# Weight maxima ahead of their scale, the second batch beside the conversion, and q by whole rows, in a linear-attention and two-layer feed-forward kernel

## The chip, the cores and the metric

The kernel runs on one core of a Trainium2 chip, as one program. The metric is the device time of that program in microseconds; several runs are taken and their median counts. TensorE (PE in the profile), VectorE (DVE), ScalarE (ACT), GpSimd (POOL) and the DMA queue of SyncE (SP) are programmed side by side. Each works through its own instructions in order and waits for the others by semaphores.

## The reference

```
q, k, v: (8 batches, 8 heads, 576, 64) f32      g_norm: (64)
kv  = einsum('bhsd,bhse->bhde', k, v)
out = einsum('bhsd,bhde->bhse', q, kv)
out = out / sqrt(mean(out * out, axis=-1) + 1e-6) * g_norm
x   = out.transpose(0, 2, 1, 3).reshape(4608, 512)
h = x @ w_in   (512 x 2048);  g = max(0.01 * h, h);   x = g @ w_out   (2048 x 512)
h = x @ w2_in  (512 x 2048);  g = h - tanh(h);        x = g @ w2_out  (2048 x 512)
```

The four weight matrices, w1 to w4 in the kernel, come as 64-bit floats. They are read as pairs of 32-bit words.

## The kernel before

**Products.** Each of the four large products works on 2 x 2 blocks by the seven-product scheme (`NOP = 7`). An operand has seven forms, four sums of blocks and three plain blocks. Each form is split into a high and a low float16 part, and three matmuls, high by high, high by low and low by high, stand for one float32 matmul. In the first product there are 64 steps (8 batches of 576 tokens by 8 pairs of weight blocks), and a step is 7 products of 6 matmuls of 288 columns, all recorded at line 513 as `ps_a` to `ps_d`. The stationary operand is a weight tile `w`. The moving one is `opa`, the three plain forms of x, or `ops`, the four sums of x, each in two halves of the contracted dimension (`kk` 0 and 1). Of the first three products that PE issues in the stream, two read `opa` and the third reads `ops`.

**Attention.** Heads go in pairs, four pairs to a batch. A pair loads k, v and q, and then PE makes kv of two heads (`pk`, 12 matmuls of 64 columns, each head in its own 64 of the 128 output partitions), transposes q in two halves (`pq`, three transposes each, both heads at once), multiplies (`po`, two matmuls of 288 columns in float32), and for every second pair sums the squares (`pm`, four matmuls of 288 columns, each in its own 32 output partitions). ACT and DVE move the results from PSUM. Batch 0 and three pairs of batch 1 run ahead of the first product. The other 25 pairs are cut into six steps that stand between products of the first 64 steps. After a batch's four pairs its root mean squares go through ACT (`iv`, L929), DVE (reciprocal, L937), DRAM and back broadcast over partitions (`bc`), and POOL scales x with them (L952). Then come high and low parts of `opa` (L452, L459), sums on POOL (L491) and the parts of `ops`.

**w1.** Its 16 units of 128 x 512 are loaded as words (L315), ACT takes absolute values of the high words (L329), and DVE takes their maximum (L333) and builds float32 from the words (L340, L346, L352). The maximum over all 16 units gives one power-of-two scale: DVE reduces (L265 to L274), PE transposes `pt` and broadcasts `pb`, DVE ends with `s1g` (L280). Only then are w1's parts made: per unit ACT makes the high and DVE the low part of three plain blocks (128 x 384), POOL makes the four sums in place, ACT and DVE split them (128 x 512; L378, L381). The other weights take the same way during the earlier products, through DRAM.

**Order.** `Plan` is a list of events by planned time with guessed durations. `on_pe` lays PE's work end to end from `plan.pe`, which starts at `START`; `chain` and `do` fit the others into free time of their engine. Instructions are issued in the order of planned times, so the plan decides each engine's order and the hardware the times. `FIRST` and `OFFS` say at which count of products the steps of a pair are put in:

```
    START = last + 45.0
    FIRST = {1: (-18.0, -11.5, -5.0, 5), 2: (18, 29, 39, 50), 3: (64, 75, 86, 97)}
    OFFS = (1, 4, 6, 8, 10, 13)
    order += [("w",) + u for u in UNITS[4:]]
    D_KV, D_Q, D_O, D_M = 0.9, 0.5, 0.6, 0.7
```

## Time and profile before

| | us |
|---|---|
| median of 3 runs | 1518.32 (1515.48 to 1521.1) |
| the profiled execution's own time | 1515.43 |
| its span | 1513.7 |
| PE busy | 1440.1 (95%) |
| DVE busy | 1248.8 (83%) |
| ACT busy | 914.5 (60%) |
| POOL busy | 687.4 (45%) |
| busy share of PE in the first two slices of 37.8 us | 5 and 2 tenths |

Shares are of the span. A matmul's record reaches from its start to its modelled end and overlaps the next one, so a busy PE is not a PE at its peak; the distance of two starts is what one costs in a row. All times in the text are microseconds from the span's start.

### The profile page before, as it was taken

To read this page: it belongs to the slowest core of one execution; us is meant where nothing else is said; L and a number is where in the kernel's file an instruction comes from. 1 tells how busy PE (TensorE), PEld (TensorE's weight loads), DVE (VectorE), ACT (ScalarE), POOL (GpSimd) and SP (SyncE) were. 2 spreads that over 40 slices of the span, in tenths; PEclk is the share of its full clock that TensorE was granted. 3 is DMA by queue.
4 is the path that set the end of the run, shared out by engine and by line. 5 is a ranking of instruction groups with operands and counts; after the bars stand their busy time and mean duration, and the time that the engine had idled before them with its cause. 6 is when DMAs were issued, how large, how long until landed. Compare 5 with 4: busy or idle time off the path is not lost. (4 is left out here: it accounts for less than half of the span.)

```text
span 1513.7 us, 32951 instructions
## 1 busy us (share of the span) xinstructions
PE 1440.1 (95%) x12658; PEld 1192.3 (79%) x12658; DVE 1248.8 (83%) x2019; ACT 914.5 (60%) x1525; POOL 687.4 (45%) x646
## 2 busy tenths in 40 slices
PE   5299999999899999999999999999998999999998
PEld 3167777777677777777777888888887888888887
DVE  4885777787777899999997888978999988888871
ACT  5377777777667645445543677778887554445540
POOL 0474330452542455445442355558885643444430
PEclk8589999999999999999999999999999999999999
DMA  9829998999978845555645866546768644444431
GB/s 265 202 62 249 289 297 247 312 281 328 305 243 283 327 154 186 199 176 176 202 162 189 320 220 211 205 169 223 266 246 300 240 156 144 146 147 141 143 96 36
DMA packets 188926, 323.17 MB, mean 214 GB/s; under 512 B 54112, under 2 KB 130912, under 8 KB 188768
## 3 DMA queue, kind: packets, MB, share of 16 engines
q1 hardware_dynamic: 188768, 321.06, 65.9%
q8 instruction: 99, 1.62, 0.4%
q14 instruction: 59, 0.48, 0.1%
HBM read 190.84 MB, written 130.15 MB: 212 GB/s over the span
## 5 line engine op out<-in xcount | busy, mean ns | idle before, releaser
L513 PEld LDWEIGHTS <-w 128*128 128x128 f16 x8400 | 819.6, 98 | 204.0 <-issue 29.7
L491 POOL TENSOR_TENSOR gl<-gl 128x256 f32<-128x256 f32 (+1 forms) x272 | 297.0, 1094 | 368.9 <-DVE gl L491 142.2
L513 PE MATMUL ps_a<-ops,w 128*128 128x288 f16 (+1 forms) x2400 | 330.9, 282 | 6.7 <-ACT u L564 4.8
L513 PE MATMUL ps_c<-ops,w 128*128 128x288 f16 (+1 forms) x2352 | 315.3, 282 | 12.2 <-DVE g L575 12.2
L513 PE MATMUL ps_a<-opa,w 128*128 128x288 f16 (+1 forms) x2016 | 283.8, 281 | 0.2
L513 PEld LDWEIGHTS <-ops 128*128 128x128 f16 x1728 | 169.1, 98 | 21.6 <-issue 2.0
L513 PE MATMUL ps_b<-opa,w 128*128 128x288 f16 (+1 forms) x1200 | 175.5, 283 | 0.0
L491 DVE TENSOR_TENSOR gl<-gl 128x256 f32<-128x256 f32 (+1 forms) x272 | 151.5, 558 | 4.3
L1249 POOL TENSOR_TENSOR g<-g,th 128x512 f32<-128x512 f32 x72 | 113.3, 1574 | 82.1 <-ACT th L1246 68.8
L513 PEld LDWEIGHTS <-opa 128*128 128x128 f16 x1296 | 126.8, 98 | 14.7
L461 DVE SCALAR_TENSOR_TENSOR ops<-gl,inv,ops 128x1024 f16<-128x1024 f32 x72 | 102.9, 1429 | 29.4 <-ACT ops L454 29.3
L952 POOL TENSOR_TENSOR xg<-xg,bc 128x1152 f32<-128x1152 f32 x16 | 47.4, 2967 | 174.7 <-DMA bc<-iv 125.7
L454 ACT ACTIVATE ops<-gl,inv 128x1024 f16<-128x1024 f32 x72 | 82.4, 1144 | 62.9 <-POOL gl L491 62.9
L452 ACT ACTIVATE ops<-gl 128x1152 f16<-128x1152 f32 x64 | 74.3, 1161 | 74.8 <-POOL gl L491 72.8
L575 DVE SCALAR_TENSOR_TENSOR g<-ps_c,u 128x288 f32<-128x288 f32 x128 | 58.1, 454 | 50.3 <-PE ps_c L513 48.5
L459 DVE TENSOR_TENSOR ops<-gl,ops 128x1152 f16<-128x1152 f32 x64 | 93.5, 1461 | 4.8 <-ACT ops L452 4.7
L513 PE MATMUL ps_c<-w,ops 128*128 128x256 f16 x864 | 97.3, 273 | 0.2 <-DVE osb L575 0.2
L513 PE MATMUL ps_a<-w,ops 128*128 128x256 f16 x864 | 95.8, 273 | 1.4 <-ACT c L566 1.4
L566 ACT ACTIVATE u<-ps_a,up 128x256 f32<-128x256 f32 x144 | 68.1, 473 | 47.1 <-PE ps_a L513 43.4
L378 ACT ACTIVATE wo<-unit,s_w 128x384 f16<-128x384 f32 (+1 forms) x96 | 63.1, 662 | 52.3 <-DVE unit L392 45.5
L491 POOL TENSOR_TENSOR x1g<-x1g 128x256 f32<-128x256 f32 x72 | 65.3, 908 | 49.4 <-DVE opa L461 43.0
L381 DVE SCALAR_TENSOR_TENSOR wo<-unit,s_w,wo 128x384 f16<-128x384 f32 (+1 forms) x96 | 84.8, 891 | 1.6 <-ACT wo L378 1.4
(126 smaller groups left out, 2171.0 us busy)
## 6 DMA issues: line engine op xcount, KB each, us to landing
g<-g SPq DMA_DIRECT2D x64, 576.0 KB, 6.4
gl<-g SPq DMA_DIRECT2D x64, 576.0 KB, 4.7
g<-g SPq DMA_DIRECT2D x72, 512.0 KB, 3.3
gl<-g SPq DMA_DIRECT2D x72, 512.0 KB, 4.4
wd<-wo SPq DMA_DIRECT2D x48, 448.0 KB, 3.3
w<-wd SPq DMA_DIRECT2D x24, 896.0 KB, 7.4
words<-in_moe_w_in_dram SPq DMA_DIRECT2D x64, 256.0 KB, 6.2
words<-in_moe_w_out_dram SPq DMA_DIRECT2D x64, 256.0 KB, 4.8
```

The lines of the kernel that those rows point to most:

```text
L378: nc.scalar.activation(out=dst()[:, 0, a:b], in_=cols(0, n), func=AF.Identity, scale=scale())
L381: nc.vector.scalar_tensor_tensor(out=dst()[:, 1, a:b], in0=cols(0, n), scalar=scale(), in1=dst()[:, 0, a:b], op0=ALU.mult, op1=ALU.subtract,)
L452: nc.scalar.activation(out=o, in_=i_, func=AF.Copy)
L454: nc.scalar.activation(out=o, in_=i_, func=AF.Identity, scale=scale())
L459: nc.vector.tensor_tensor(out=o, in0=i_, in1=h, op=ALU.subtract)
L461: nc.vector.scalar_tensor_tensor(out=o, in0=i_, scalar=scale(), in1=h, op0=ALU.mult, op1=ALU.subtract)
L491: lambda: e.tensor_tensor(out=g()[:, o], in0=g()[:, a], in1=g()[:, b], op=op),
L513: nc.tensor.matmul(out=out_, lhsT=a, rhs=c, start=start and m == 0, stop=stop and m == n - 1, skip_group_check=not fresh,)
L566: nc.scalar.activation(out=t, in_=src, func=AF.Identity, scale=self.scale)
L575: nc.vector.scalar_tensor_tensor(out=o, in0=src, scalar=self.minus if sub else self.scale, in1=t, op0=ALU.mult, op1=ALU.add,)
L952: e.tensor_tensor(out=x, in0=x, in1=held[kk].ap[:, n0:n1], op=ALU.mult)
L1249: e.tensor_tensor(out=g()[:, n], in0=g()[:, n], in1=held["t"].ap[:, n], op=ALU.subtract)
```

## The change

- **q** is loaded like k and v, two heads in one DMA of 1536-byte rows, where two DMAs of 256-byte runs stood. Since the heads are now apart, each half of q is turned by six float32 matmuls with the identity, three for each head, which write the head's own 64 partitions (`tile_position`), where three transposes of both heads stood.
- **w1, scale.** Units of blocks 5, 6 and 7 (`LATE`, 6 of 16) no longer go through the conversion ahead of the scale: DVE takes their maximum from the words (`most`), and the words stay in their buffers; absolute value, clamp, shift and the two joins come after the scale. Units of blocks 0 and 1 (`SOON`) have their sums made by POOL ahead of the scale.
- **All weights, parts.** The seven forms lie side by side in one float32 unit (128 x 896). The sums are made in float32 first, then ACT makes all high parts in one instruction and DVE all low parts in one, where two of each stood (`parts`; the form numbers in `PROD` follow).
- **Batch 0** has its reciprocal in one instruction of 288 columns, and its broadcast by eight float32 matmuls of 288 columns with a 0-1 matrix (`wide`), from which DVE scales x; its sums of x are made by DVE as well. DRAM, POOL and the two broadcasting loads are left out for this batch.
- **Batch 1.** Its first pair is loaded ahead of w1's last two units, the others right behind them. Three pairs still stand ahead of the product stream, the fourth at its head, and later pairs 3 or 4 products earlier. `START` is no longer 45 us behind the last pair of batch 0, but behind the third of batch 1.
- **Plan.** Where a product was planned before what it needs, the kernel stopped; now a trial run of the plan finds out by how much and delays PE's planned time there. No instruction comes of that. The guessed duration of half a q (0.5) is unchanged.

```diff
-PROD = {1: (6, 5), 2: (4, 4), 3: (0, 6), 4: (5, 0), 5: (3, 1), 6: (1, 2), 7: (2, 3)}
+PROD = {1: (6, 4), 2: (4, 3), 3: (0, 5), 4: (5, 0), 5: (3, 1), 6: (1, 2), 7: (2, 6)}
...
+    def count(n):
+        converted[n] += 1
+        if converted[n] == 2 * NP:
+            weight_scale(n, plan.now + 1.0)
+
+    def convert(n, i, kk, t, land, keep=None, later=None, then=()):
...
+        def most():
+            nc.vector.tensor_reduce(
+                out=mw[:, n, 2 * i + kk:2 * i + kk + 1], in_=held["w"].ap[:, 1::2].bitcast(F32), axis=AX.X, op=ALU.max,
+                apply_absolute_value=True,
+            )
+            count(n)
+
+        def clamp():
+            o = held["ap"]
+            nc.vector.tensor_scalar(out=o, in0=o, scalar1=LEAST_HIGH, scalar2=None, op0=ALU.max)
+
+        if later is not None:
+            plan.chain(t, [(None, land, load), ("V", 0.65, most)])
+            later.append([
+                (None, 0.0, room), ("A", 0.7, one), ("V", 0.42, clamp), ("V", 0.42, shift), ("V", 0.69, low), ("V", 0.69, high),
+            ])
+            return
...
+    def sums(w, minus4, merged=False):
...
+    def parts(w, dst, scale):
+
+        def cols():
+            return w().rearrange("p (o c) -> p o c", c=P)
+
+        def hi():
+            nc.scalar.activation(out=dst()[:, 0], in_=cols(), func=AF.Identity, scale=scale())
+
+        def lo():
+            nc.vector.scalar_tensor_tensor(
+                out=dst()[:, 1], in0=cols(), scalar=scale(), in1=dst()[:, 0], op0=ALU.mult, op1=ALU.subtract,
+            )
+
+        return [("A", 1.15, hi), ("V", 1.25, lo)]
...
-            apart = nm != "q"
-            held[nm] = L.take([CP, 2, NC, D] if apart else [CP, NC, 2, D], F32, nm)
-            if apart:
-                nc.sync.dma_start(
-                    out=held[nm].ap.rearrange("p h c d -> p h (c d)"),
-                    in_=src[b, 2 * c:2 * c + 2].rearrange("h (p c) d -> p h (c d)", p=CP),
-                )
-                continue
-            for h in range(2):
-                nc.sync.dma_start(out=held[nm].ap[:, :, h], in_=src[b, 2 * c + h].rearrange("(p c) d -> p c d", p=CP))
+            held[nm] = L.take([CP, 2, NC, D], F32, nm)
+            nc.sync.dma_start(
+                out=held[nm].ap.rearrange("p h c d -> p h (c d)"),
+                in_=src[b, 2 * c:2 * c + 2].rearrange("h (p c) d -> p h (c d)", p=CP),
+            )
...
-                nc.tensor.transpose(
-                    qt[r][0][:, CP * a:CP * a + CP], two_heads(held["q"], r * NC // 2 + a), ident[:CP, :CP]
-                )
+                for h in range(2):
+                    nc.tensor.matmul(
+                        out=qt[r][0][D * h:D * h + D, CP * a:CP * a + CP], lhsT=held["q"].ap[:, h, r * NC // 2 + a],
+                        rhs=ident[:CP, :CP], start=True, stop=True, tile_position=(0, D * h), skip_group_check=True,
+                    )
...
+        def wide(kk, n):
+            k_ = (4 * kk + n) % 4
+            if k_ in used:
+                raise NoRoom("bank")
+            held["b", kk, n] = bank(k_, "pb")
+            nc.tensor.matmul(
+                out=held["b", kk, n][:, :T1], lhsT=hot["t"].ap[:, kk, n], rhs=held["iv"], start=True, stop=True,
+            )
+
+        def scale_wide(kk, n):
+            x = xg[b, kk].ap[:, n]
+            nc.vector.tensor_tensor(out=x, in0=x, in1=held["b", kk, n][:, :T1], op=ALU.mult)
+            free((4 * kk + n) % 4)
...
+            if b == 0:
+                for kk in range(2):
+                    for n in range(4):
+                        plan.chain(
+                            plan.now + 0.2 + 0.7 * (4 * kk + n),
+                            [(None, 0.9, lambda kk=kk, n=n: wide(kk, n)), ("V", 0.46, lambda kk=kk, n=n: scale_wide(kk, n))],
+                        )
+                return
...
+    SOON = (0, 1)
+    LATE, EARLY, GAP = (5, 6, 7), 3, 0.0
...
-        order += [("w",) + u for u in UNITS[hp:hp + 1]]
-    order += [("w",) + u for u in UNITS[4:]]
-    ta = {}
+        order += [("w",) + u for u in UNITS[2 * hp:2 * hp + 2]]
+    order += [("w",) + u for u in UNITS[8:14]] + [("a", 1, PAIRS[0])] + [("w",) + u for u in UNITS[14:]]
+    order += [("a", 1, PAIRS[hp]) for hp in range(1, 4)]
...
+            later = after_scale.setdefault(o[1:], []) if o[1] in LATE else None
+            convert(0, o[1], o[2], t, 5.5, place_w1(o[1], o[2]), later, sums_first(*o[1:]) if o[1] in SOON else [])
...
+                plan.chain(plan.now + 1.3 * kk, ([] if i in SOON or i in LATE else sums_first(i, kk)) + split_first(i, kk))
...
+            if i in LATE:
+                for kk in range(2):
+                    last_ = [(None, 0.0, lambda i=i: pair_(i))] if kk else []
+                    when(
+                        ("w", 0, i - 3, 0), plan.now + 0.3 + STEP * (i - 1) + 2.3 * kk,
+                        lambda i=i, kk=kk, last_=last_: plan.chain(plan.now, after_scale[i, kk][0] + sums_first(i, kk) + last_),
+                    )
+                continue
...
-    START = last + 45.0
+    last = ta[1, PAIRS[0]][0]
+    for hp in range(EARLY):
+        early_pair(1, PAIRS[hp], last + 0.8, ta[1, PAIRS[hp]][1])
+        last += 6.0
+    START = last + GAP
...
-    FIRST = {1: (-18.0, -11.5, -5.0, 5), 2: (18, 29, 39, 50), 3: (64, 75, 86, 97)}
...
+    FIRST = {1: (None,) * EARLY + (0, 8, 16, 24)[:4 - EARLY], 2: (14, 25, 36, 47), 3: (60, 72, 84, 96)}
+    OFFS = {1: (0, 2, 3, 4, 6, 8)}
```

On PE, ahead of the product stream, the rows of before from w1's scale to the third pair of batch 1 (`pt` and the first `pb` are the scale's, `kvd` the two heads' kv):

```order
L234 MATMUL pt<-ident,m_w_690 1x128
L834 MATMUL pk<-v,k 64x64 x12
L244 MATMUL pb<-diag_w_708,ones 128x1
L854 MATMUL pq<-ident,q 128x96 x6
L870 MATMUL po<-qt,kvd_325 128x288 x2
L834 MATMUL pk<-v,k 64x64 x12
L854 MATMUL pq<-ident,q 128x96 x6
L870 MATMUL po<-qt,kvd_326 128x288 x2
L907 MATMUL pm<-sq,sel 32x288 x4
L834 MATMUL pk<-v,k 64x64 x12
L854 MATMUL pq<-ident,q 128x96 x6
L870 MATMUL po<-qt,kvd_325 128x288 x2
```

The same place now (`pb<-iv,hot` is the broadcast of batch 0; four more of these and the first pair's `pk` and `pq` stand ahead of the first row):

```order
L1096 MATMUL pb<-iv,hot 128x288
L992 MATMUL po<-qt,kvd_327 128x288
L1096 MATMUL pb<-iv,hot 128x288
L992 MATMUL po<-qt,kvd_327 128x288
L1096 MATMUL pb<-iv,hot 128x288
L329 MATMUL pt<-ident,m_w_750 1x128
L1096 MATMUL pb<-iv,hot 128x288
L954 MATMUL pk<-v,k 64x64 x12
L339 MATMUL pb<-diag_w_765,ones 128x1
L975 MATMUL pq<-ident,q 64x96 x12
L992 MATMUL po<-qt,kvd_328 128x288 x2
L1029 MATMUL pm<-sq,sel 32x288 x4
```

One pair of batch 1 moved from behind the scale's `pt` to ahead of it, and seven of the eight broadcasts stand ahead of it too.

In the product stream, one half of a q among products on PE, before:

```order
L513 LDWEIGHTS w_0_746
L513 MATMUL ps_c<-ops,w_0_746 128x288
L854 MATMUL pq<-ident,q 128x96 x3
L513 LDWEIGHTS w_2_825
L513 MATMUL ps_a<-opa,w_2_825 128x288
```

And now:

```order
L637 LDWEIGHTS w_0_814
L637 MATMUL ps_a<-ops,w_0_814 128x288
L975 MATMUL pq<-ident,q 64x96 x6
L637 LDWEIGHTS w_1_863
L637 MATMUL ps_a<-opa,w_1_863 128x288
```

Three instructions on all 128 output partitions became six on 64 of them, alone between products. There are 50 such places in the stream before and after.

On DVE, the last 12 rows up to the second half of the low parts of `ops` before:

```order
L459 TENSOR_TENSOR ops<-xg,ops 128x576
L381 SCALAR_TENSOR_TENSOR w_0_746<-w1f_388,s1g,w_0_746 128x384
L459 TENSOR_TENSOR ops<-xg,ops 128x576
L381 SCALAR_TENSOR_TENSOR w_1_780<-w1f_469,s1g,w_1_780 128x384
L381 SCALAR_TENSOR_TENSOR w_0_746<-w1f_388,s1g,w_0_746 128x512
L885 COPY xg<-po 128x288
L381 SCALAR_TENSOR_TENSOR w_1_780<-w1f_469,s1g,w_1_780 128x384
L885 COPY xg<-po 128x288
L381 SCALAR_TENSOR_TENSOR w_2_825<-w1f_527,s1g,w_2_825 128x384
L459 TENSOR_TENSOR ops<-xg,ops 128x576
L381 SCALAR_TENSOR_TENSOR w_0_746<-w1f_388,s1g,w_0_746 128x512
L459 TENSOR_TENSOR ops<-xg,ops 128x576
```

And now (L614 is a sum of x, L519 a low part of w1, L473 the clamp of a late unit, L705 takes a product's result out of PSUM):

```order
L614 TENSOR_TENSOR xg<-xg 128x288 x2
L705 SCALAR_TENSOR_TENSOR g<-ps_b,c_926 128x288
L519 SCALAR_TENSOR_TENSOR w_1_863<-w1f_462,s1g,w_1_863 128x896
L614 TENSOR_TENSOR xg<-xg 128x288
L581 TENSOR_TENSOR ops<-xg,ops 128x576
L519 SCALAR_TENSOR_TENSOR w_2_949<-w1f_541,s1g,w_2_949 128x896
L581 TENSOR_TENSOR ops<-xg,ops 128x576
L519 SCALAR_TENSOR_TENSOR w_2_949<-w1f_541,s1g,w_2_949 128x896
L581 TENSOR_TENSOR ops<-xg,ops 128x576
L473 TENSOR_SCALAR w1f_966<-w1f_966 128x512
L519 SCALAR_TENSOR_TENSOR w_3_971<-w1f_602,s1g,w_3_971 128x896
L581 TENSOR_TENSOR ops<-xg,ops 128x576
```

The low parts of w1 stand among the parts of `ops` as before, now in whole units, and the sums of x have come to DVE; the first result of a product is taken out ahead of the first low part of `ops`. From `s1g` to the last of these rows DVE has 7 low parts of w1 (128 x 896), 8 sums of x, 2 low parts of `opa` of 288 and 2 of 576 columns, 4 of `ops` of 576, 4 copies, 1 scaling of x, 1 result of a product and 1 clamp.

## Rows read from the trace of the kernel before

**Rows 1.** PE, what precedes the products: start, length, instruction, idle before and its releaser
```profile
64.91 0.37 PE L234 MATMUL pt<-ident,m_w 128*1 128x128 f32 x1 [29.18 <-DVE m_w L274]
71.45 1.55 PE L834 MATMUL pk<-v,k 96*64 96x64 f32 x24
...
84.69 1.65 PE L513 MATMUL ps_a<-opa,w 128*128 128x288 f16 x6
86.13 1.59 PE L513 MATMUL ps_b<-opa,w 128*128 128x288 f16 x6
87.61 0.65 PE L513 MATMUL ps_a<-ops,w 128*128 128x288 f16 x4
```
**Rows 2.** ACT and POOL in the same stretch
```profile
45.15 0.66 ACT L329 ACTIVATE w1f<-words 128x512 f32<-128x512 f32 x1 [0.76 <-DMA words<-in_moe_w_in_dram]
55.17 8.71 POOL L952 TENSOR_TENSOR xg<-xg,bc 128x1152 f32<-128x1152 f32 x2 [53.86 <-DMA bc<-iv]
```
**Rows 3.** DVE in the same stretch
```profile
39.52 0.75 DVE L937 RECIPROCAL iv<-iv 128x96 f32<-128x96 f32 x1
...
64.12 0.16 DVE L265 TENSOR_REDUCE m_w<-mw 128x1 f32<-128x16 f32 x1
...
68.44 0.75 DVE L280 TENSOR_TENSOR s1g<-s_w,gcol 128x1 f32<-128x1 f32 x1
...
81.28 0.75 DVE L381 SCALAR_TENSOR_TENSOR w<-w1f,s1g,w 128x512 f16<-128x512 f32 x1 [0.17 <-ACT w L378]
81.95 1.28 DVE L459 TENSOR_TENSOR ops<-xg,ops 128x576 f16<-128x576 f32 x1
...
86.49 0.46 DVE L885 COPY xg<-po 128x288 f32<-128x288 f32 x1 [1.40 <-ACT sq L876]
```
**Rows 4.** Stretches: their ends, length, busy time by engine, granted clock, DMA share, GB/s
```profile
30.00:44.00 14.00, 4.45 (x15) 1.81 (x15) 13.84 (x34) 10.14 (x20) 0.00 (x0) 0.50 1.04 332
64.90:80.60 15.70, 14.51 (x106) 9.26 (x106) 12.56 (x22) 9.13 (x21) 13.37 (x17) 0.50 0.77 157
391.30:398.10 6.80, 5.70 (x26) 3.87 (x26) 6.73 (x12) 5.92 (x14) 5.30 (x6) 0.50 1.15 273
```
**Rows 5.** PE in the product stream, near 97 us
```profile
97.00 0.41 PE L854 MATMUL pq<-ident,q 96*128 96x96 f32 x3
97.25 0.90 PE L513 MATMUL ps_c<-ops,w 128*128 128x288 f16 x6
97.99 0.90 PE L513 MATMUL ps_b<-opa,w 128*128 128x288 f16 x6
98.72 0.65 PE L870 MATMUL po<-qt,kvd 128*128 128x288 f32 x2
99.21 0.90 PE L513 MATMUL ps_a<-ops,w 128*128 128x288 f16 x6
```
**Rows 6.** PE in the product stream, near 150 us
```profile
148.28 0.90 PE L513 MATMUL ps_a<-ops,w 128*128 128x288 f16 x6
149.11 0.69 PE L907 MATMUL pm<-sq,sel 128*32 128x288 f32 x8
149.74 0.91 PE L513 MATMUL ps_a<-opa,w 128*128 128x288 f16 x6
150.48 0.90 PE L513 MATMUL ps_c<-ops,w 128*128 128x288 f16 x6
151.31 0.92 PE L834 MATMUL pk<-v,k 96*64 96x64 f32 x24
152.16 0.91 PE L513 MATMUL ps_a<-opa,w 128*128 128x288 f16 x6
```
**Rows 7.** Group of PE's instructions from 84.6 to 600 us: count, busy, mean ns
```profile
L854 PE MATMUL pq<-ident,q 96*128 96x96 f32 x150 | 21.2, 250 | 0.0
```
**Rows 8.** Later stretches, columns as in rows 4
```profile
168.00:480.00 312.00, 302.28 (x2706) 232.82 (x2704) 238.57 (x446) 223.93 (x442) 117.03 (x116) 0.99 0.92 286
1120.00:1200.00 80.00, 71.89 (x635) 62.64 (x634) 78.29 (x103) 55.98 (x85) 49.82 (x42) 0.98 0.83 295
```
**Rows 9.** PE and ACT around 390 us
```profile
392.24 1.12 PE L513 MATMUL ps_a<-ops,w 128*128 128x288 f16 x4 [4.13 <-ACT u L564]
390.41 0.92 ACT L452 ACTIVATE opa<-xg 128x864 f16<-128x864 f32 x1 [7.56 <-DMA wf<-unit]
```
**Rows 10.** DMA from 5 to 29 us
```profile
DMA packets 9589, 6.48 MB, mean 270 GB/s; under 512 B 5046, under 2 KB 9588, under 8 KB 9588
```

More of the change, by code (lines that the diff above doesn't have):

```diff
@@ L111, in on_pe, with go, miss, met @@
     def on_pe(self, dur, fn):
-        self.at(self.pe, fn)
+        k = self.ops
+        self.ops += 1
+        self.pe += self.delays.get(k, 0.0)
+        def go():
+            self.op = k
+            fn()
+            self.op = None
+        self.at(self.pe, go)
         self.pe += dur
         return self.pe
+    def miss(self, key):
+        if not self.dry or self.op is None and self.first is None:
+            raise AssertionError(("planned too late", self.now, key))
+        if self.first is None:
+            self.first = self.op, key, self.now
+        raise Missed
+    def met(self, key):
+        if self.first and self.first[1] == key:
+            raise Resolved
     def run(self):
@@ L189, in body, with done @@
     done_ = set()
+    def done(*what):
+        for x in what:
+            done_.add(x)
+            plan.met(x)
     def need(what):
-        assert what in done_, ("planned too late", plan.now, what)
+        if what not in done_:
+            plan.miss(what)
     def when(what, t, fn):
@@ L440, in load_weights, with left_stages @@
         )
-    def left_stages(g, dst, scale, T, done=None, first=None, pieces=1, rest=None, gps=None):
+    def left_stages(g, dst, scale, T, over=None, first=None, pieces=1, rest=None, gps=None):
         f = T / 1000.0
@@ L502, in part @@
         kind = "A" if a >= 4 else "S"
-        assert kind in ops.get("ready", ""), ("planned too late", plan.now, kind)
+        if kind not in ops.get("ready", ""):
+            plan.miss(("part", id(ops), kind))
         return ops["A"].ap[:, h, a - 4] if a >= 4 else ops["S"].ap[:, h, a]
@@ L546, in bank @@
             need = {6: "c1", 7: "u2", 3: "22", 4: "u3" if self.one4 else None}.get(p)
-            assert need is None or need in self.done, ("planned too late", plan.now, need)
+            if need is not None and need not in self.done:
+                plan.miss((id(self), need))
             start = p in (1, 2, 5) or p == 4 and not self.one4
@@ L584, in add @@
             if which != "c" or blk == "12":
-                used.discard(self.banks[which])
+                free(self.banks[which])
             if self.ready:
@@ L595, in add_alone @@
             for which in "bc":
-                used.discard(self.banks[which])
+                free(self.banks[which])
             if self.ready:
```

277 lines of the change are left out of this document (161 added, 116 removed).

## The prediction

> **What bounds the kernel now.** I read the stretches first, then PE's timeline, then what PE waits for. From the first product at 84.69 to the end PE hardly rests, so the time is the start of that stream plus what stands in it. In the stream PE is idle in two places worth naming: 312 less 302.28, that is 9.7 us, between 168 and 480 us, and 8.1 us between 1120 and 1200 [rows 8].
>
> Ahead of the stream PE is bound by order and by others. The last words of w1 are there at 45.15 [rows 2], but DVE first finishes all conversions and then stands behind POOL, which scales batch 0's x from 55.17 for 8.71 us [rows 2]; so w1's scale begins at 64.12 [rows 3]. Its transpose starts on PE at 64.91 after 29.18 us of idleness, and three pairs of batch 1 follow at the lower level of the clock (0.50 of 2.4 GHz is 1.2 GHz, [rows 4]), so that the first product comes at 84.69 and the third, the first that needs `ops`, at 87.61 [rows 1]. The two products ahead of it are 86.13 less 84.69 and 87.61 less 86.13, 1.44 and 1.48 us apart, twice the 0.74 us of a product at full clock (149.74 to 150.48, [rows 6]).
>
> **The change, part 1: the head of the stream.** The order of DVE keeps its reciprocal where it was, at 39.52 [rows 3]; three pieces of 0.75 us in one, less what each piece needs to start, are some 2.1 us, so PE can begin the broadcasts at 41.6. A float32 matmul of 288 columns costs 0.49 us at full clock (98.72 to 99.21, [rows 5]), so 0.98 us at half, at which the clock stands after so long a rest [rows 4]. Seven broadcasts (6.9 us) and a pair (at most 71.45 less 64.91, 6.5 us, with two small matmuls of the scale in it, [rows 1]; 6.0 taken) stand ahead of `pt`: 54.5 us. The words are no bound: with one pair of batch 1 (0.885 MB, 2.7 us at 332 GB/s, [rows 4]) ahead of the last two units they land by 48 us. From `pt` to `s1g` it was 64.91 to 68.44 plus 0.75, 4.3 us [rows 1, 3]; a broadcast and a `pk` now stand in between, 1.0 and 1.5 us: `s1g` at 61.3. Two pairs follow on PE, 6.5 us each at half the clock and half of it at full, so the first product starts at 65 to 71, middle 67.5, against 84.69.
>
> That is not yet the gain, for the third product waits for `ops`. From `s1g` to there DVE has 30 instructions in its order: 7 low parts of 896 columns, of which no row exists (0.75 us for 512 [rows 3], in proportion 1.31; 1.15 taken, since part of an instruction is fixed), 8.0 us; 16 of 288 columns at 0.46 [rows 3], 7.4 us; 6 of 576 columns, 1.28 with POOL at work beside DVE [rows 3], twice 0.46 as the low end, 0.8 taken because POOL has no work of batch 0 now, 4.8 us; the clamp 0.45. That is 20.7 us, and the records overlap by 0.08 (81.28 plus 0.75 against 81.95, [rows 3]), 2.4 us over 30: 18.3 us. The third product comes at 79.5, 8 us earlier than 87.61. The dear prices give 83.5 (4 us earlier), a clock back at full level by 50 us gives 76 (12 earlier). PE rests for some us before that, and the trace shows what such a rest does: after 4.13 us of idleness [rows 9] the granted clock was 0.50 from 391.3 to 398.1 [rows 4], worth 3.4 us. PE's rest here is broken by the fourth pair's `pk` and the first half of the product; I charge 0.5 (0 to 3.4). **Head: -7.5 us, from -12 to -1.**
>
> **Part 2: q in the stream.** Half a q costs the stream 0.25 us now (97.00 to 97.25, [rows 5]). The new form, two heads side by side in halves of the output partitions, is that of `pk`, and `pm` is its relative in quarters. `pm` takes from 148.28 plus 0.74, 149.02, to 149.74, 0.72 us, for four matmuls of 288 columns [rows 6]; one costs 0.49, so the four run side by side, and 0.23 us goes for getting in and out. `pk` takes from 150.48 plus 0.74, 151.22, to 152.16, 0.94 us [rows 6]; less 0.23, 0.71 us for six slices of two heads, 0.118 each for 64 columns (0.49 by 64/288 is 0.109: two heads in the time of one). With 96 columns a slice is 0.177, three are 0.53, and with 0.23 a half costs 0.76. There are 150 transposes in the stream, 50 halves [rows 7], each between products, so each pays the 0.23: 50 times 0.51 is **+25.5 us**. PE does not rest there, so nothing hides it. Bounds: without the 0.23, 50 times 0.28, +14; with the heads one after the other, 6 times 0.177 and 0.23, 1.29, +52.
>
> The Trainium skill speaks to both sides of this. Its page "TensorEngine Tiling (Array Packing)" has under "Theoretical Speedup" up to twofold speed for a dimension of 64 or less, by which alone a half would be three slices and the change +14; under "Key Properties" it says that a change of the tiling mode drains TensorE, without a price. The rows side with the second: 0.23 us is left over in `pm` and in `pk` alike.
>
> **Part 3: what the stream gets back.** Between 168 and 480 us PE is idle for 9.7 us, and the stretch at half clock costs 3.4 more [rows 4, 8]: 13.1 us to be had. DMA is busy for 0.92 of it [rows 8], and the longest rest, 4.13 us, ends behind an ACT that stood 7.56 us for a store to free a buffer [rows 9]. q's 256-byte runs weigh there. From 5 to 29 us, 6.48 MB were moved in 24 us [rows 10], 4608 of the 5046 short packets being q's 1.18 MB; the other 5.3 MB take 16.0 us at 332 GB/s [rows 4], which leaves up to 8 us for a batch's q, against 3.6 at that rate. Six batches give back up to 26 of 287 us of DMA time, an estimate from these rows. Besides, the same products now take PE some two thirds of 25.5 us longer there, time in which ACT, DVE and DMA catch up. I take **-11 us**, from -13.1 to 0.
>
> **Part 4: edits at nothing.** The conversion that the six late units bring to DVE behind `s1g` (four instructions each, at most 0.75 us, [rows 3]: 18 us) is hidden by the first 49 products and five pairs, 49 times 0.74 and five of 3.8, 55 us, before the last weights are used; with 9 low parts (10 us) and some 21 results of products (10 us) DVE has 38 us of work in them. Without that cover it would be up to +8. Sums of w1 on POOL lie beside the conversion. The parts in one instruction spare ACT and DVE a start each in 48 later units; PE covers that, but for the 8.1 us at 1120 to 1200 us, where DVE is busy for 78.29 of 80 [rows 8]: 0, at best -8.
>
> **Sum.** The profiled execution took 1515.43 us, 2.9 less than the median of the three runs. 1515.4 - 7.5 + 25.5 - 11 is **1522 us**, 0.25% over the median. Half a per cent, 7.6 us, is about what a measurement of this kernel tells from no change: 1510.7 to 1525.9 is no change.
>
> **Rivals.**
> - *Getting in and out is free* where 96 columns hide it: 1522 less 11.5, 1511. Against it: two groups of different length show the same 0.23. The section on speedup of the Trainium skill's page, taken alone, leads here.
> - *The idle time stays.* The new order of DVE and ACT keeps buffers as long as before, and PE stands at 388 us, or at like places, behind ACT again: 1522 plus 11, 1533, slower. For it: ACT's wait of 7.56 us needs only one store that comes late. It decides from the point where less than 7.5 of the 13.1 us come back.
> - *The heads take turns* (the identity is read by both): 1549. `pk` speaks against it.
> - *`ops` is ready in time*, and the stream starts whole at 67.5, its third product at 69: 18.6 us earlier instead of 8, 1511.5. Against it: DVE's order.
> - *The rest at 1120 to 1200 us goes too*: 1514.
>
> **How the numbers follow.** The forecast has 0.46, free entry 0.13, staying idle time 0.20, heads in turn 0.05, early `ops` 0.10, the last 0.06. The forecast's own range is 1514 to 1530. Up to 2 in 10 left out, the cases reach from 1506 to 1538. Faster by over half a per cent: a little under half of the two cases at 1511 and the tails of the others, 0.18. Slower: 0.18 of the 0.20, the heads in turn, and a quarter of the forecast, 0.36. Same: 0.46.
>
> **What would show it.** In the changed kernel's profile: first product at 65 to 71 and the third at 76 to 84, with DVE without a gap between `s1g` and the last low part of `ops`; 0.76 us from the end of the product ahead of a `pq` to the next; PE's idle time between 168 and 480 us down to 2 us and no stretch of half clock there; a lower DMA share. The prediction fails if a `pq` costs under 0.6 or over 0.9 us, if PE rests as long as before in the stream, or if new waits come up behind late weights before 140 us.

## The result and the profile after

The changed kernel took 1528.5 us (median of 6 runs, 1525.51 to 1532.29) against 1521.07 for the kernel before in the same runs (6, 1515.48 to 1525.91): a ratio of **1.0062 [1.0043, 1.0081]**, slower by a little over half a per cent. The forecast was 1522 (1506 to 1538). By the prediction's own half per cent this is slower, to which it gave 0.36, and not the same, to which it gave 0.46. The profiled execution took 1527.58 us, 12.1 more than that of before; the prediction's sum gave 7 more. The profiled execution of before, 1515.43, was as fast as the fastest of the six runs beside it, so 12.1 is more than all runs together show: 7.4 us between the medians, 9.4 by the ratio.

From the page of the changed kernel: its span, busy time by engine with instructions, PE's clock in 40 slices, the DMA total.

```profile
span 1525.8 us, 33919 instructions
PE 1471.8 (96%) x13250; PEld 1209.1 (79%) x13250; DVE 1247.6 (82%) x1971; ACT 908.0 (60%) x1461; POOL 676.8 (44%) x636
PEclk9789999999999999999999999999999999999999
DMA packets 156464, 321.89 MB, mean 211 GB/s; under 512 B 16656, under 2 KB 98448, under 8 KB 156304
```

PE is busy for 31.7 us more than before, in a span 12.1 us longer. Bytes are nearly the same; the packets under 512 B fell from 54112 to 16656, by q's 37 thousand.

PE's timeline at the head of the stream (answers to [rows 1]):

```profile
58.82 0.27 PE L329 MATMUL pt<-ident,m_w 128*1 128x128 f32 x1
...
70.78 0.94 PE L637 MATMUL ps_a<-opa,w 128*128 128x288 f16 x6
71.91 0.92 PE L954 MATMUL pk<-v,k 96*64 96x64 f32 x24 [0.20 <-DVE xg L1007]
72.76 0.91 PE L637 MATMUL ps_b<-opa,w 128*128 128x288 f16 x6
74.56 0.28 PE L637 MATMUL ps_a<-ops,w 128*128 128x288 f16 x1 [0.89 <-ACT ops L574]
77.02 0.93 PE L637 MATMUL ps_a<-ops,w 128*128 128x288 f16 x3 [2.17 <-DVE ops L581]
80.48 0.64 PE L637 MATMUL ps_a<-ops,w 128*128 128x288 f16 x2 [2.54 <-DVE ops L581]
81.05 1.23 PE L975 MATMUL pq<-ident,q 96*64 96x96 f32 x12
82.21 1.62 PE L637 MATMUL ps_a<-opa,w 128*128 128x288 f16 x6
```

DVE's timeline there (to [rows 3]):

```profile
43.99 1.94 DVE L1059 RECIPROCAL iv<-iv 128x288 f32<-128x288 f32 x1
...
57.08 0.16 DVE L360 TENSOR_REDUCE m_w<-mw 128x1 f32<-128x16 f32 x1
...
63.18 0.15 DVE L375 TENSOR_TENSOR s1g<-s_w,gcol 128x1 f32<-128x1 f32 x1
...
66.17 0.46 DVE L1007 COPY xg<-po 128x288 f32<-128x288 f32 x1 [0.94 <-ACT sq L998]
...
80.69 1.14 DVE L519 SCALAR_TENSOR_TENSOR w<-w1f,s1g,w 128x896 f16<-128x896 f32 x1
81.75 0.75 DVE L581 TENSOR_TENSOR ops<-xg,ops 128x576 f16<-128x576 f32 x1
```

The first product starts 13.9 us earlier (70.78 against 84.69). The third starts at 74.56 behind ACT's part of `ops` and is cut in three by two waits for DVE's low parts. Products run without such waits from the fourth on, at 82.21, where before it was 88.34: a gain of 6.1.

PE in the stream (to [rows 5, 6]):

```profile
147.47 0.90 PE L637 MATMUL ps_a<-opa,w 128*128 128x288 f16 x6
148.30 0.72 PE L975 MATMUL pq<-ident,q 96*64 96x96 f32 x12
148.95 0.91 PE L637 MATMUL ps_c<-ops,w 128*128 128x288 f16 x6
```

From 147.47 plus 0.74, 148.21, to 148.95: 0.74 us for half a q. Over all 50 halves the median is 0.742; before it was 0.250.

To compare stretches I use the start of the n-th of the 11,424 product matmuls, counted from 0: number 18 is the first of the fourth product, number 2500 lies behind the last of q's halves, and where the expectations below say product 100, 600 or 2500 they mean this count. Stretches of the changed kernel from number 18 to 2500, on to 6000, on to 9000, and then the stretch of [rows 8] (columns as in [rows 4]):

```profile
82.20:488.80 406.60, 401.33 (x3858) 299.87 (x3857) 299.24 (x542) 283.39 (x541) 146.02 (x144) 1.00 0.82 256
488.80:914.70 425.90, 422.68 (x3509) 343.02 (x3508) 394.38 (x610) 225.24 (x307) 194.56 (x158) 1.00 0.62 213
914.70:1256.50 341.80, 331.21 (x3006) 294.58 (x3004) 302.92 (x448) 245.97 (x392) 224.50 (x201) 1.00 0.64 224
168.00:480.00 312.00, 306.73 (x2948) 229.79 (x2947) 233.33 (x425) 217.64 (x414) 114.05 (x111) 1.00 0.87 277
```

Of the prediction's signs in that last stretch, no half clock came (1.00) and the DMA share fell, 0.87 for 0.92; PE's idle time fell from 9.7 to 5.3 us, not to 2.

I call PE's *rest* its idle time plus half the time at the lower clock, and PE's *work* what is left of the stretch. All profiled executions, in us (an execution's span is 1.8 below its time). Each row is one execution, the ratio is of all runs. The executions lie within 2.5 us of the median of their kernel's runs, that of before 3 to 6 us below the medians of its runs (1518.3 to 1521.1). So a difference of a few us of rest between two rows is shown only where the ratios show it too:

| kernel | no. 18 | no. 2500 | work, rest between | 6000 to 9000 | span | ratio to before |
|---|---|---|---|---|---|---|
| before | 88.3 | 479.7 | 376.2, 15.1 | 339.1 | 1513.7 | |
| changed | 82.2 | 488.8 | 399.3, 7.3 | 341.8 | 1525.8 | 1.0062 [1.0043, 1.0081] |
| 1 changed, q as before | 79.3 | 481.5 | 374.8, 27.3 | 342.3 | 1518.4 | 0.9996 [0.9977, 1.0014] |
| 2 before, q as changed | 87.2 | 493.3 | 401.3, 4.8 | 338.7 | 1527.9 | 1.0082 [1.0063, 1.0102] |
| 3 changed, short runs | 82.6 | 493.5 | 398.9, 12.0 | 341.8 | 1531.0 | 1.0084 [1.0061, 1.0106] |
| 4 changed, one group | 84.7 | 485.6 | 388.1, 12.8 | 342.0 | 1522.9 | 1.0045 [1.0021, 1.0069] |
| 5 long rows, old transposes | 77.6 | 477.1 | 375.0, 24.4 | 341.3 | 1514.1 | 0.9964 [0.9951, 0.9978] |
| 6 changed, parts in two | 81.3 | 493.0 | 399.7, 12.0 | 341.5 | 1529.0 | 1.0069 [1.0055, 1.0083] |
| 7 changed, w1 pairs later | 78.2 | 497.5 | 399.1, 20.2 | 342.4 | 1535.6 | 1.0121 [1.0108, 1.0134] |
| 8 three edits together | 76.0 | 490.2 | 374.6, 39.6 | 341.8 | 1526.1 | 1.0070 [1.0052, 1.0089] |
| 9 as 1, norms' loads together | 78.8 | 471.5 | 376.2, 16.5 | 341.6 | 1508.7 | **0.9959 [0.9945, 0.9973]** |
| 10 as 6, late order of before | 83.1 | 495.8 | 399.6, 13.1 | 338.8 | 1529.7 | one run, none |
| 11 changed, norms' loads together | 82.0 | 485.3 | 399.2, 4.0 | 341.6 | 1521.8 | 1.0025 [1.0013, 1.0036] |
| 12 before, norms' loads together | 89.7 | 482.5 | 377.1, 15.8 | 338.7 | 1516.4 | 1.0005 [0.9990, 1.0019] |

The work takes three values whatever else is changed: 375 to 377 us with q's old transposes, 399 to 401 with the new, 388 with the grouped ones. What differs beyond that is rest. From number 9000 to the start of the last it is 264.9 us in every one.

### The profile page after: what moved, and what is told of

Its sections match the earlier page's. It is cut to its first block, busy times and chain, and to the rows that moved or that the text cites. A ratio compares the mean times of both kernels' runs of the same rounds, so it can differ in the third digit from the quotient of the medians.

```text
span 1525.8 us, 33919 instructions
## 1 busy us (share of the span) xinstructions
PE 1471.8 (96%) x13250; PEld 1209.1 (79%) x13250; DVE 1247.6 (82%) x1971; ACT 908.0 (60%) x1461; POOL 676.8 (44%) x636
## 2 busy tenths in 40 slices
DMA packets 156464, 321.89 MB, mean 211 GB/s; under 512 B 16656, under 2 KB 98448, under 8 KB 156304
## 5 line engine op out<-in xcount | busy, mean ns | idle before, releaser
L614 POOL TENSOR_TENSOR gl<-gl 128x256 f32<-128x256 f32 (+1 forms) x272 | 299.6, 1102 | 365.4 <-DVE gl L614 147.6
L614 DVE TENSOR_TENSOR gl<-gl 128x256 f32<-128x256 f32 (+1 forms) x272 | 151.9, 560 | 4.7
L705 DVE SCALAR_TENSOR_TENSOR g<-ps_c,u 128x288 f32<-128x288 f32 x128 | 57.9, 452 | 60.4 <-PE ps_c L637 60.1
L1074 POOL TENSOR_TENSOR xg<-xg,bc 128x1152 f32<-128x1152 f32 x14 | 38.9, 2778 | 146.0 <-DMA bc<-iv 100.7
L614 POOL TENSOR_TENSOR x1g<-x1g 128x256 f32<-128x256 f32 x72 | 66.7, 929 | 48.6 <-DVE opa L583 45.3
L581 DVE TENSOR_TENSOR opa<-gl,opa 128x864 f16<-128x864 f32 x64 | 80.6, 1259 | 2.9 <-ACT opa L574 2.5
L705 DVE SCALAR_TENSOR_TENSOR g<-ps_c,up,u 128x256 f32<-128x256 f32 x144 | 65.3, 475 | 18.3 <-PE ps_c L637 12.1
```

The lines of the kernel that those rows point to most:

```text
L581: nc.vector.tensor_tensor(out=o, in0=i_, in1=h, op=ALU.subtract)
L614: lambda: e.tensor_tensor(out=g()[:, o], in0=g()[:, a], in1=g()[:, b], op=op),
L705: nc.vector.scalar_tensor_tensor(out=o, in0=src, scalar=self.minus if sub else self.scale, in1=t, op0=ALU.mult, op1=ALU.add,)
L1074: e.tensor_tensor(out=x, in0=x, in1=held[kk].ap[:, n0:n1], op=ALU.mult)
```

## The experiments

**1. The changed kernel with q's old two loads and transposes.**

```diff
-    nc.sync.dma_start(out=held[nm].ap.rearrange("p h c d -> p h (c d)"), in_=src[b, 2 * c:2 * c + 2]...)
+    for h in range(2):
+        nc.sync.dma_start(out=held[nm].ap[:, :, h], in_=src[b, 2 * c + h].rearrange("(p c) d -> p c d", p=CP))
...
-    for h in range(2): nc.tensor.matmul(... tile_position=(0, D * h) ...)
+    nc.tensor.transpose(qt[r][0][:, CP * a:CP * a + CP], ..., ident[:CP, :CP])
```

> The changed kernel with q loaded and transposed as before (two loads of 256-byte runs, three transposes a half); all else is the change. Theory: each half of a q by heads costs the stream 0.74 us against 0.25, so 50 halves give back 24.6 us, and the DMA traffic of the short runs takes some 8 us of idle time back: about 1511 us, ratio 0.990 to 0.998 against the kernel before, and PE idle between 150 and 480 us up from 5 to about 10 us or more. Rival: the new q hides in time in which PE waits anyway, and the loss is elsewhere: 1528 us, ratio 1.005. Second rival: nothing is taken back: 1503 us, ratio 0.987.

0.9996: the time of before. PE's work fell by 24.5 us, the time by 7.4 by the spans and by 10 by the two ratios. In the trace 20 us went into rest, which is now 27.3, nearly twice that of before, in a kernel whose stream starts 9 us earlier: number 2500 comes at 481.5, later than before's 479.7. What holds it shows at the longest rest. The timelines of SP's queue, POOL, ACT and PE of this kernel:

```profile
145.74 1.27 SPq L1072 DMA_DIRECT2D bc<-iv  x2
147.10 0.55 SPq L784 DMA_DIRECT2D g<-g  x1
147.75 0.38 SPq L461 DMA_DIRECT2D wf<-unit  x1
148.22 1.18 SPq L940 DMA_DIRECT2D k<-in_k_dram  x1
149.50 1.16 SPq L940 DMA_DIRECT2D v<-in_v_dram  x1
150.75 1.37 SPq L946 DMA_DIRECT2D q<-in_q_dram  x2
152.17 2.13 SPq L1072 DMA_DIRECT2D bc<-iv  x2
...
152.37 3.06 POOL L1078 TENSOR_TENSOR xg<-xg,bc 128x1152 f32<-128x1152 f32 x1 [25.82 <-DMA bc<-iv]
163.42 2.61 POOL L1078 TENSOR_TENSOR xg<-xg,bc 128x1152 f32<-128x1152 f32 x1 [7.98 <-DMA bc<-iv]
...
166.06 0.92 ACT L574 ACTIVATE opa<-xg 128x864 f16<-128x864 f32 x1 [7.88 <-POOL xg L1078]
...
167.33 1.32 PE L637 MATMUL ps_a<-ops,w 128*128 128x288 f16 x6 [4.34 <-ACT u L694]
```

A batch's norms are broadcast by two pairs of loads, one per half of the contracted dimension. The second pair stands behind six other transfers and lands some 10 us after it was issued. POOL waits for it, ACT waits for POOL with PE's results queued behind `opa`, and PE stops. The rest is paid twice: with these 4.34 us and 2.05 more at 171 the granted clock fell to 0.50, 1.2 GHz, from 167.7 to 174.5 us.

**2. The kernel before with q as changed**, loads and transposes alone, the reverse of the diff above.

> The kernel before with the new q alone (one load of 1536-byte rows, six matmuls a half). Theory: 24.6 us more in the stream, some 4 us more for the three pairs of batch 1 ahead of it at half clock, some 8 us of idle time given back: ratio about 1.013, and the first product 3 to 6 us later than 84.7. Rival: the new q costs nothing: 1.000. If nothing is given back: 1.018.

1.0082: less than the price of the transposes alone, for the rest fell from 15.1 to 4.8. So q alone gets some 10 us back without any other edit. Not as expected, the first product came 1.4 us earlier than before (83.27), not 3 to 6 later; what made it earlier is open. Against this kernel the changed one is 5 us ahead at number 18 and 4.5 at 2500, so in these two traces the head's gain arrives nearly whole with the dear transposes; the ratios, 1.0082 and 1.0062, are 3 us apart and their intervals overlap.

**3. The changed kernel with q loaded in runs of 256 B,** into rows padded to 72 so that the runs stay apart; PE's matmuls unchanged.

```diff
-    held[nm] = L.take([CP, 2, NC, D], F32, nm)
+    held[nm] = L.take([CP, 2, NC, D + 8 * short], F32, nm)
...
+    for h in range(2):
+        nc.sync.dma_start(out=held[nm].ap[:, h, :, :D], in_=src[b, 2 * c + h].rearrange("(p c) d -> p c d", p=CP))
```

> The changed kernel with q loaded in two DMAs of 256-byte runs again, into rows padded from 64 to 72 elements, and the matmuls by heads kept: the work of PE is that of the change, the DMA traffic that of before. Theory that long rows took the idle time away: PE idle between 168 and 489 us goes from 5 us back to 10 or more, ratio 1.009 to 1.012. Rival, that a longer PE time took it away (other engines have more time for the same products): idle time stays at about 5 us and the ratio at 1.006.

1.0084, between the two theories. In the trace the work is unchanged and the rest 4.7 us higher (12.0 against 7.3). By the ratios long rows are worth 3 us here, with intervals that overlap. In the traces, from run 1's 27.3, the dear transposes alone take the rest down to 12.0, the rows then to 7.3.

**4. The changed kernel with `pk` and both halves of q in one group,** so that PE enters and leaves the narrow form once a pair, not three times.

```diff
-            qt[r] = att_bank("pq")
+            qt[r] = att_bank("pq") if r else (held["pk"], held["bank"])
...
-            for (dur, fn, after), o in zip(pair(b, c, held), OFFS.get(b, (1, 4, 6, 8, 10, 13))):
+            for (dur, fn, after), o in zip(pair(b, c, held), OFFS.get(b, (4, 4, 4, 8, 10, 13))):
```

> The changed kernel with kv and both halves of q of a pair issued one behind the other (kv and the first half share a PSUM bank, the places of the steps in the stream follow). The instructions are the same. Theory that getting in and out of the halves of the array costs 0.23 us a group: 25 pairs save two groups each, 11.5 us, a group of pk and two pq takes 0.94 plus two times 0.51, 1.96 us in place of 2.43, ratio 0.996 to 1.001. Rival, that the price lies in each matmul: 2.43 us, ratio 1.006.

PE's timeline of this kernel (the first half of q is recorded under the name of the bank it shares, `pk`, L974):

```profile
101.98 0.90 PE L637 MATMUL ps_a<-ops,w 128*128 128x288 f16 x6
102.81 0.92 PE L954 MATMUL pk<-v,k 96*64 96x64 f32 x24
103.56 0.67 PE L974 MATMUL pk<-ident,q 96*64 96x96 f32 x12
104.06 0.67 PE L974 MATMUL pq<-ident,q 96*64 96x96 f32 x12
104.66 0.91 PE L637 MATMUL ps_c<-ops,w 128*128 128x288 f16 x6
```

From 102.72 to 104.66 the group costs 1.94 us, the median of all 25 as well. Less 0.944 for `pk`, a half in a group is 0.50 where it was 0.742 alone: 0.245 for each entry and exit, which the prediction had as 0.23. The Trainium skill, "TensorEngine Tiling (Array Packing)", section "Key Properties", says that a change of the tiling mode drains TensorE. The 0.245 us agrees with that, and is what it costs here. The price was right, the gain was not: of 11.3 us of work saved, 5.5 went into rest and 2.5 were lost at the head.

**5. Long rows with the old transposes:** the loads of the changed kernel, but three transposes of 128 contiguous columns a half.

```diff
-    for h in range(2): nc.tensor.matmul(... lhsT=held["q"].ap[:, h, r * NC // 2 + a] ...)
+    nc.tensor.transpose(qt[r][0][:, CP * a:CP * a + CP], flat[:, P * m:P * m + P], ident[:CP, :CP])
```

> The changed kernel with q loaded in its rows of 1536 B, but with one transpose of 128 contiguous columns for three slices a half, as PE did before. Two rows of one head then stand where two heads should, so this kernel computes something else than the reference; its transfers are those of the change and its PE time is that of before. The last run with q's old loads and transposes ended at a span of 1518.4 us although PE had 24.6 us less to do, since idle time of 23 us came up before product 2500 (481.5 us there). Theory 1 (transfers): q's short runs hold up the loads behind them; with the rows, product 2500 comes at 470 to 475 us, the span is 1508 to 1512, ratio 0.993 to 0.996. Theory 2 (the chain from the sum of squares through store, broadcast load, POOL, ACT and DVE sets the pace, however q is loaded): product 2500 at 480 to 482, span 1517 to 1519, ratio 0.999 to 1.000.

Number 2500 at 477.1 and 0.9964: between the theories. Against run 1 it is 1.7 us ahead at number 18 and 4.4 at 2500. Runs 3 and 5 agree on 3 to 5 us for the transfers, by the ratios too (0.0022 and 0.0032 of 1519 us). The rest is still 24.4, so q's short runs hold little of run 1's 27.3.

**6. Parts of later units in two instructions,** as before. In this kernel, in run 8 and in run 10 one column block of each later unit gets its parts ahead of its sum, so they compute something else than the reference; number and size of the instructions are those of before.

```diff
-        stages = sums(lambda: held["u"].ap, n == 2, n == 2)
-        stages += parts(lambda: held["u"].ap, lambda: held["o"].ap, lambda: small[f"s_{name}"])
+        stages = parts(*args_, 3, NOP) + sums(args_[0], n == 2, n == 2) + parts(*args_, 0, 3)
```

> The changed kernel with the parts of the 48 later units made in two instructions again: columns that need no sum first, then POOL's sums, then the rest. Behind product 6000 the changed kernel loses 2.7 us against before (0.5 at product 7600, 1.2 at 7900, 0.9 behind 8200), at the second place with ACT 2.94 us behind a sum of x on POOL, with sums of weight units standing closer together ahead of it. Theory: the order that the one-piece parts give POOL makes this; without it the loss falls to under 0.7 us, the span to 1523 us, ratio 1.004. Rival: it comes from the other order of the products' operands, and 2 to 3 us of loss stay, ratio 1.006.

The theory fell as put: from 6000 to 9000 it takes 341.5 us, 2.3 above before. And number 2500 came 4.1 us later than in the changed kernel, with 12.0 of rest. New among the waits is that POOL's sums of units wait for DVE's first low parts. The waits from 85 to 480 us of this kernel (engine, tile and line that waited, what for; us in total, times, longest):

```profile
POOL unit L496 <- DVE wo L519: 58.3, 9, 22.6
```

In this trace one instruction in place of two, which I had priced at nothing, would be worth 4 to 5 us between numbers 18 and 2500. The ratios of all runs, 1.0069 and 1.0062, do not tell the two kernels apart, so neither that gain nor that this wait makes it is shown.

**7. The second and third pair of w1 planned 6 us later.**

```diff
-    STEP, LAG = 4.2, 1.0
+    STEP, LAG = 4.2, 7.0
```

> The changed kernel with one number changed: the second and third pair of w1 are planned 6 us later behind the scale, so that DVE makes the last low parts of ops ahead of them. Theory (the stream's fourth product waits for DVE's order, not for DVE's amount of work): product 18 comes at 78 to 80 us instead of 82.2. What of these 3 us arrives at product 2500 is the second question: all of it if PE sets the pace there (span 1522.5, ratio 1.004), little of it if the chain of the norms does (span 1525, ratio 1.006). Rival: the products behind the first 49 now wait for w1, and product 100 comes no earlier than 97.5 us.

Number 18 came at 78.2 as the theory had it, 4.0 us earlier, and the kernel was slower, 1.0121. The rival's wait came, later than it said. PE of this kernel:

```profile
113.90 0.30 PE L637 MATMUL ps_a<-opa,w 128*128 128x288 f16 x1 [2.11 <-DVE w L519]
124.03 0.66 PE L637 MATMUL ps_a<-opa,w 128*128 128x288 f16 x2 [2.66 <-ACT w L516]
```

PE waits for parts of w1, and the clock was 0.50 for 6.8 us from the second of these waits on. Between matmuls 100 and 300 this kernel loses 11.5 us to the changed one. The 38 us of DVE's work that the prediction hid behind the first products is hidden with less than 6 us to spare.

**8. q's old form, parts in two and the w1 pairs later, together.**

> The changed kernel with q's old loads and transposes, the parts of later units in two instructions and the second and third pair of w1 planned 6 us later: the versions of the three parts that the runs and traces so far speak for. If the late loss goes and what the head gains is again lost before 480 us, the span is 1515 to 1516, ratio 0.997 to 0.998; if the head's gain arrives too, 1511 to 1513, ratio 0.995 to 0.996. Against it: the new order meets waits of its own, ratio 1.000 or above.

1.0070: no gain of the three arrived; 39.6 us of rest. What runs 6 and 7 cost may both be in it; this run does not part them.

**9. Run 1 with both pairs of the norms' loads behind each other.**

```diff
-                plan.chain(plan.now + 1.8 + 3.0 * kk, more[kk])
+                plan.chain(plan.now + 1.8 + 0.2 * kk, more[kk])
```

> The changed kernel with q's old loads and transposes, and for the batches behind the first with both pairs of broadcast loads of the norms right behind each other in SP's queue, where a store of g and of a unit, k, v and q's two loads stood between them. In the run without this, the second pair's load was issued at 152.2 us with DMA busy for more than its share, POOL stood 7.98 us for it, ACT behind POOL 7.88 us, PE 4.34 and 2.05 us, and products 500 to 600 took 7 us longer than before. Theory (the place of the second pair in the queue makes this rest): the wait of 7.98 us goes, product 600 comes at 176 to 178 us instead of 183.0, and if nothing later takes it back the span is 1511 to 1513, ratio 0.995 to 0.997. Rival (transfers as a whole set the pace): k, v, q and the words come later by what the norms come earlier, the rest goes to another place before product 2500, which stays at 479 to 482 us; span 1516 to 1519, ratio 0.999 to 1.000.

**0.9959 [0.9945, 0.9973]**: faster than before and than the changed kernel, and 5.6 us faster than run 1 by the two ratios. The timeline of SP's queue and POOL of this kernel, then its stretch from number 18 to 2500:

```profile
145.36 2.60 SPq L1072 DMA_DIRECT2D bc<-iv  x4
...
152.32 5.27 POOL L1078 TENSOR_TENSOR xg<-xg,bc 128x1152 f32<-128x1152 f32 x2 [26.32 <-PE ps_a L637]
```

```profile
78.80:471.50 392.70, 380.77 (x3417) 292.20 (x3415) 302.36 (x543) 278.25 (x542) 150.15 (x144) 0.99 0.87 265
```

POOL's two scalings stand together, the wait of 7.98 us is gone, number 600 comes at 174.8 where it was 183.0. The work is that of run 1 within 1.4 us, the rest 16.5 instead of 27.3. The DMA share is 0.87 as in run 1, and number 2500 comes at 471.5, where the rival had 479 to 482: transfers as a whole do not set the pace. The edit plans the whole chain of the second half earlier, its scaling and its parts as well. But between numbers 18 and 2500 PE and POOL have the same order as in run 1, and ACT and DVE differ in a few instructions only; so it is the place of one pair in the queue.

**10. Run 6 with the planner's costs of these steps as before,** which puts the instructions of POOL, and with them those of ACT and DVE, in the second layer back into the order of before.

```diff
-        f = 0.28 if merged else 0.6
+        f = 0.28 if merged else 0.5
...
+        f = {3: (0.74, 0.78), 4: (0.62, 0.62), 7: (1.15, 1.25)}[b - a]
```

> The changed kernel with the parts of later units in two instructions and with the planner's costs of these steps as before, which gives POOL word for word the order of before from its first sum of the second layer's x on. One column block of each later unit gets its parts ahead of its sum, so this kernel computes something else than the reference; the instructions and their times are those of a right one. Theory (POOL's order makes the late loss): from product 6000 to product 9000 it takes 339.1 us as before, against 341.8 in the changed kernel and 341.4 with two instructions alone. Rival (the loss is in something else): 341 to 342 us.

338.8 us from 6000 to 9000, as before. The late loss is the planned order: in this stretch POOL, ACT and DVE each have the order of before in run 10, and each another one in run 6, with PE's the same in all. That POOL's order is the one that counts is read from the rows of the changed kernel, not shown by the run:

```profile
1115.42 2.71 POOL L614 TENSOR_TENSOR x1g<-x1g 128x256 f32<-128x256 f32 x2
1118.10 0.72 POOL L496 TENSOR_TENSOR unit<-unit 128x256 f32<-128x256 f32 x1
1118.78 1.85 POOL L614 TENSOR_TENSOR x1g<-x1g 128x256 f32<-128x256 f32 x2
...
1119.98 1.15 ACT L576 ACTIVATE ops<-x1g,s_x 128x1024 f16<-128x1024 f32 x1 [2.94 <-POOL x1g L614]
...
1121.55 0.81 PE L637 MATMUL ps_a<-ops,w 128*128 128x256 f16 x6 [1.08 <-ACT u L696]
```

POOL has no gap here, and a sum of a weight unit stands between those of x. ACT stands 2.94 us for the sum of x behind it with PE's result queued behind `ops`, and PE 1.08. In run 10 ACT makes these `ops` without a wait.

**11. The changed kernel with the norms' loads together,** the edit of run 9.

> The changed kernel with q as changed, and both pairs of broadcast loads right behind each other in SP's queue. Theory (with q's dearer transposes PE is behind the chain of the norms anyway): only the rest of 2.32 us at 174.5 us can go, product 2500 comes at 486 to 489 us, ratio 1.005 to 1.006. Rival (loads pushed back bring new rests): product 2500 at 490 us or later, ratio 1.007 or above.

Better than expected: the rest falls from 7.3 to 4.0 and the ratio from 1.0062 to 1.0025. The one long rest of the changed kernel's stretch, 2.32 us at 174.5, was the same chain. Its POOL names another releaser, and the queue tells better:

```profile
158.61 1.24 SPq L1068 DMA_DIRECT2D bc<-iv  x2
...
169.04 2.63 POOL L1074 TENSOR_TENSOR xg<-xg,bc 128x1152 f32<-128x1152 f32 x1 [6.53 <-PE ps_a L637]
...
176.84 0.41 PE L637 MATMUL ps_c<-ops,w 128*128 128x288 f16 x2 [2.32 <-DVE g L705]
```

The second pair of loads, issued from 158.61, took up to 9.6 us to land, until 168.8, just ahead of POOL's start at 169.04. In run 11, with the same order on PE, POOL scales both halves in one go from 160.17 to 165.8, so no product of PE held it.

**12. The kernel before with the norms' loads together.**

> The kernel before with one edit: both pairs of the norms' broadcast loads right behind each other in SP's queue, as in the run with q's old loads that took 0.996 of the time before. It tells how much of that run is the queue's and how much is the head's. Theory (the queue edit only lets the head's gain arrive; before, the chain of the norms is hidden by a later start of the stream): product 2500 at 477 to 480 us, span 1511 to 1514, ratio 0.998 to 1.000. Rival (the queue edit is worth as much without the head): product 2500 at 470 to 473 us, span 1504 to 1508, ratio 0.993 to 0.996.

1.0005: worth nothing there, with 15.8 us of rest as before. Before, the second pair's place costs nothing: the stream starts later, and other waits take the same time. That the later start is the reason is argued, not shown.

## Why the prediction was right, and where not

- **Head, -7.5 (-12 to -1): right.** Measured -6.1. `s1g` came at 63.18 for 61.3, the low part of 896 columns took 1.14 for 1.15, and DVE took 19.2 us to the end of the last low part of `ops`, for 18.3, with one gap of 0.94 us behind ACT at 66.17 where the prediction had none. That `s1g` came so near is in part luck: DVE's reciprocal started at 43.99, not at 39.52, and `pt` at 58.82, not at 54.5, but from `pt` to `s1g` it took 4.5 us, not 6.8. The forecast's order of events, two products, a third that stalls behind DVE, is in the rows. The lower clock after it lasted to 86.2, so that 2.0 us of rest, not 0.5, belong to this wait. Run 7 shows that DVE's order made the wait; it also shows that this order is needed.
- **q in the stream, +25.5: right.** Half a q took 0.742 for 0.76; work rose by 23.1 us in the stretch, with 49 of the 50 halves in it. Of the 0.492 more, 0.245 is entry and exit, which run 4 took away; the other half is that three slices in the narrow form take 0.50 where three wide transposes took 0.25. A slice of 0.166 is what a float32 matmul of 96 columns costs (0.49 by 96/288, [rows 5]). The Trainium skill, "TensorEngine Tiling (Array Packing)", section "Restrictions", lists transpose mode for FP32 among what column tiling disables; no run here tries a transpose in the narrow form. The rivals of free entry and of heads in turn fall.
- **What the stream gets back, -11: the picture was off, the size is not settled.** In the two traces it was -7.8 (rest 15.1 to 7.3). On average of all runs more came back: the other terms below add up to 20.0, and the whole was 7.4 to 9.4, which leaves 10.6 to 12.6, an estimate, since those terms are of one trace each. I had taken the 13.1 us of before as a fixed amount, with q's transfers as its first cause and the slower PE besides. It is not fixed: run 1, with the head earlier and q cheap, has 27.3, and there the chain of the norms makes 10.8 of it (run 9). In the kernel before it is not that chain, for moving its loads leaves 15.8 (run 12), and the longest rest stands behind a store [rows 9]. The transfers are worth 3 to 5 us (runs 3 and 5); counted from run 1, 15.3 of 20 came back by the slower PE alone (run 3). More comes by moving two loads (run 11). The rival of idle time that stays decided at 7.5 us come back, and 7.8 did in the traces: it was near.
- **Edits at nothing: this step failed.** It had 0 for one instruction of parts in place of two, at best -8 at 1120 to 1200 us. There the edits cost 2.7 us from matmul 6000 to 9000, by the planned order: two instructions alone do not undo it (run 6, 341.5), with the old guessed durations as well they do (run 10, 338.8). The nine runs from the changed kernel other than run 10 have 341.3 to 342.4 there, the two from the kernel before 338.7. A gain of it between numbers 18 and 2500 (run 6) is not shown. A merge of instructions, and a guessed duration in the plan, can move the instructions that the plan places behind them, on every engine; the prediction looked at DVE's and ACT's starts alone.
- **Sum.** -6.1 + 23.1 - 7.8 + 2.7, and 0.3 between 2500 and 6000, is 12.2 us; the spans differ by 12.1, as they must, since the terms come from the same two traces. Against these the forecast's 7 came 5 short: 3 in what comes back, 3 late, 1 at the head, less 2 in q. Against all runs, 7.4 to 9.4, it was near, in part by luck: q came 2.4 us cheaper than forecast, which pays for most of a late loss that the sum did not have.

What the change is worth then: all but q's part gave nothing by itself (run 1, 0.9996), since its gain at the head was lost in the stream. With the norms' loads moved it is worth 0.41% (run 9), and the loads alone nothing (run 12). q's new form costs 10 us by the ratios, with the loads moved (runs 11 and 9) and without (the changed kernel and run 1); the spans, 13.1 and 7.4, are of one execution each.

Open: what holds the 16.5 us of rest that run 9 still has in the stretch, and a kernel with run 9's queue, parts in one instruction and the late order of before, which was not tried.

## What to carry to other kernels

Do not count idle time of the bounding engine as a stock from which a change can be paid: here it grew when the engine got faster or started earlier, since another wait came next. Work out when the second chain is ready, in absolute time, and give the head start only to the point where that chain meets it; here, by the ratios, only 10 of 24.5 us less work on PE arrived in run 1, 15 of 24.3 in run 5 and some 3 of 11.3 in run 4 (each with the changed kernel; for run 4 the intervals overlap), and 10 of 23 in run 9 (with run 11). Where a plan orders all engines, an edit's price has to be read from the order it makes on every engine, POOL included. And when a long chain passes through a shared queue, look at what stands between its own transfers before counting bytes.

## What the runs showed of the hardware

- Getting PE into and out of the form with two 64-column halves costs 0.245 us for a group at full clock (run 4; 0.23 read from `pk` and `pm` before), and two float32 matmuls of 96 columns side by side take 0.166 us, the time of one (0.49 by 96/288 is 0.163).
- Idle time cost more than itself. In run 1, 17.3 us of idleness in the stretch came with three stretches at 1.2 GHz, 17 us together: another 8.5 us of work lost.
- A load of 288 KB landed after some 10 us where its median was 6.3, when the profile's DMA share was 1.04 to 1.19 (stretches of 5 us from 150 to 170 us of run 1).
